# A recurrence followed by an MLP on one core: six weight blocks finished on GpSimd, and a new order of all steps

## The chip, the cores and the metric

The kernel runs on one core of a Trainium2 chip. The core has TensorE for matrix products (PE in the profile; PEld is its loading of weights), VectorE (DVE), ScalarE (ACT), GpSimd (POOL) and SyncE (SP), which here only issues DMAs. Each engine works through its own queue in order and waits on semaphores for the others. The metric is the device time of one execution in microseconds (us), the median of several runs.

## The reference

A recurrence in the manner of RWKV-7 runs over 768 positions for 4 batches and 8 heads with a 40 x 40 state each; its outputs, 3072 tokens of 320 features, go through an MLP with an exact GELU and 2048 hidden features.

```python
for t in range(S):                       # S = 768; state is (B, H, D, D), D = 40
    y[:, :, t] = np.einsum('bhd,bhde->bhe', rt, state)
    Sa = np.einsum('bhde,bhe->bhd', state, at)
    state_decay = state * wt[:, :, None, :] - np.einsum('bhd,bhe->bhde', Sa, bt)
    state = state_decay + np.einsum('bhd,bhe->bhde', vt, kt)
...
x = attn_out.transpose(0, 2, 1, 3).reshape(B * S, H * D)   # 3072 x 320
h = x @ w_in                                               # 320 x 2048
g = 0.5 * h * (1.0 + erf(h * inv_sqrt2))
return (g @ w_out).astype(np.float32)                      # 2048 x 320
```

r, k, v, w, a and b are float32. The two weight matrices arrive as float64 and are read by the kernel as pairs of 32-bit words.

## The kernel before

The sequence is cut into 12 chunks of 64 positions. Within a chunk the recurrence is a set of matrix products and the inverse of a triangular 64 x 64 matrix for each of 32 pairs of batch and head; between chunks only the state is carried on. For chunk c the main steps are: `logs`, `sums` (cumulated logarithms of the decay, and their exponentials), `sc`, `sk` (b and k times weights), `ta`, `tb`, `tk`, `tv`, `tr` (turned operands), the products `N`, `A`, `RV`, each followed by a mask on VectorE (line 676; 703 for chunk 0), the inverse, `av`, `X`, `sa`, `saT`, `M`, and at the end `yy`, `QY`, `qk`, `y` and `state`. Two chunks are under way at any time.

The inverse of chunk 0 is made by squaring (`sq0`, `sq1` for two halves, then `cornerd`, `joinedd`): five rounds, in each of which TensorE multiplies, VectorE transposes (line 865) and adds (868), and ScalarE copies (871). For the other chunks GpSimd inverts 32 x 32 blocks with pairs of short instructions (`inv`, lines 799 and 801), about 26 us of its time for each chunk. It reads N as written to DRAM and loaded back (`nb`), and the result goes through DRAM too (`ft`); `corner` and `joined` put the blocks together.

The MLP of a chunk is `ph` (x times w_in, line 1119, then GELU on ScalarE, line 1122) and `po` (times w_out). For the first two chunks `po` is a plain product (line 1141); from then on it is one level of Strassen's scheme, seven products of half size (line 1157) with sums on VectorE and ScalarE, and two stores of two DMAs each (`store`).

The weights are converted from float64 words in the kernel itself, since the chip computes in float32: ten pieces of w_in (`ci`, 128 x 512 each) and sixteen blocks of w_out (`co`, 128 x 320 each). Each goes through `to_float` (line 452) and one of three buffers `conv0` to `conv2`: VectorE takes the exponent and mantissa bits apart (lines 457 and 458), ScalarE rebiases the exponent (461), VectorE puts the sign in (466), and two more VectorE operations add the low word to the mantissa (472) and multiply by the power (473). The tuples `POOLED_IN` and `POOLED_OUT` name the pieces for which ScalarE scales both parts instead (463, 464) and GpSimd does the addition and the multiplication (469, 470); both are empty before. The words of w_out's blocks 12 and 13 lie in the rows that later hold b and k of a chunk.

Everything that surrounds these steps is set by hand. `ORDER` is a list of tokens such as `ci4:2` or `sq0`. Each step is a generator; a token runs it to its next `yield`, and the numbers after a colon choose its buffers in PSUM (`duo0` to `duo3`) or its conversion buffer. The tokens therefore set the order of instructions in every engine's queue and of the DMAs in SyncE's. The steps of the start are `begin6` (a memset and six products that keep TensorE busy until the first data arrive), `warm0` to `warm7` (a product of constants each), `consts`, `zeros`, `pads` and `gaps` (constants on GpSimd), `tables` (a dummy logarithm or exponential, which has ScalarE load that table) and the loads: `w1` is the load of w for chunk 1, and so on; `wi`, `wl` and `wo` load the weights' words.

Of the kernel before, what the change touches and what calls it, by code (L numbers as in the profile page):

```python
# [33 lines left out]
sq1 sq0 sq1:2 k1 sq0 sq1 warm1:1 N1 sq1 sk0 ci0:0 wi0 sq1:0 N1 ci0 sq1 tr0:1 sq1 ci0 tk0:2 wi0 tk0 sk1 wi0 sq0:3 sq1  # L34
sq0 tr0 A0:2 ci1:1 sq1:0 sq0 ci1 sq1 sq0 nb1 sq1 A0 sq1 wi0 sq0:1 wi0 sq0 RV0:3 sq0 RV0 sq0 wl1 sq1:0 wl1 sq1 inv1 r2
sq0:2 sq1 sq1 sq0 tk1:1 sq0 sq0 sq1:3 tk1 w2 sq1 sq0:0 sq0 cornerd0 placed2 av0:2 ci2:2 placed3 cornerd0:3 ci1 ci2
inv1 nb1 placed1 warm0:1 cornerd0 wl0 ci3:0 wl0 av0 av0:0 r1 ci2 joinedd0:1 av0 joinedd0 tr2:3 placed0 joinedd0 tr2
warm2:2 wi1 a2 ci3 sa0:0 sa0 sa0:1 inv1 sa0 b2 warm5:2 ci4:1 ci9:2 ci4 QY0:3:0 logs2 ci4 k2 qk0 warm7:2 ci9 y0 warm3:1
wi1 state0 wi1 A1:2 wi1 A1 wi1 sums2:1 wi1 inv1 ci9 wo2 sums2:0 sums2 ci3 tv1:3 tv1 tr1:2 sc2 sums2 tn1:0 ci5:1 tn1
ta2:3 ta2 ci5 av1:1 tr1 ci5 sk2 inv1 y0:0 tb2:3 wi1 inv2 ci7:2 tb2 wo6 zeros6 y0:2 ci7 zeros7 y0 y0 tk2:3 av1 ci6:0  # L40
N2:2 ci6 N2 ft1 tk2 co3:1 ph0:0 ft1 ci6 wi1 ph0 corner1:0 N2 ci7 X1:1 corner1:2 corner1 ft1 ph0 X1 ph0:3 wo0 ci8:0
co2:2 ci8 RV1:2 RV1 nb2 warm4:1 ci8 joined1:0 wo9 joined1 wq3 ph0 co0:0 joined1 co0 inv2 ph0 co0 v2 ph0:1 co2 co3
co1:0 sa1:2 co1 sa1 w3 co1 saT1:0 saT1 co3 ph0 co2 wo4 ph0 inv2 ph0:3 co6:0 wt3:1 co6 co7:2 ph0 vp3 co7 ph0 co7
yy1:2:0 logs3 M1:1 M1 tv2:3 wt3 co6 wo8 sums3:1 nb2 sums3 wt3 QY1 zeros5 a3 inv3 tv2 qk1 co4:2 y1 wo15 po0:1 inv2
co5:0 y1 state1 co5 co4 po0 co5 RV2:3 wo10 A2:0 co4 y1 tn2:2 A2 tn2 co9:0 po0 ta3 co9 wt3 inv2 co15:2 bp3 po0 co9 co15
# [5 lines left out]
av3 sums4:1 po1 X3 po1 RV3:2 v4 ws0 sums4 N4:3 N4 inv5 sk4 RV3 ph2:1 N4 sc4 tk4:2 ph2 ft3 ph2 ft3 ph2:3 ws3 nb4 ws1
nb4 ph2 corner3:1 ph2 ft3 ph2:2 inv4 a5 corner3:1 corner3 w5 ph2 ph2 joined3:3 joined3 r4 tn3:1 joined3 tn3 inv4
saT3:3 saT3 sa3:2 sa3 logs5 po1 ph2:1 ta5 bp5 yy3:3:2 M3:0 M3 inv4 tv4 ph2 ph2 tr4 wq5 QY3 qk3 po2:0 po1 sums5:0 sums5
y3 po1 po2:1 state3 y3 po2 inv4 wt5:2 RV4:0 po2:1 po2 wt5 k5 A4:2 po2 A4 tn4:3 y3 tn4 wt5 po2:1 tables1 wt5 po2 po2
inv4 kp5 av4:2 tb5 av4 X4:3 po2 ph3:2 sk5 X4 a6 po2 ta5 ph3 v5 RV4 N5:3 N5 ws2 po2:1 N5 po2 ft4 po2 ph3 ft4 ph3:0 ft4
corner4:0 nb5 tk5:2 ph3 vp5 ph3 corner4:3 ta6 corner4 inv5 nb5 po2 po2:1 po2 joined4:2 joined4 joined4 ph3:0 b5 saT4:3
saT4 sa4:1 r5 inv5 sa4 ph3 ph3 sc5 ph3:2 w6 yy4:3:1 M4:0 M4 tv5 ph3 inv5 ph3 tr5 wq6 QY4 logs6 po3:1 qk4 bp6 state4
po3:0 kp6 y4 po3 po3:2 wt6:0 A5:2 po2 sums6:1 A5 wt6 inv6 k6 inv5 sums6 wt6 y4 po3 wt6 po3 po3:3 po3 po3 tn5:2 y4 tn5
av5:1 tb6 RV5:0 po3 av5 po3 po3:2 ta6 b6 po3 inv5 po3 a7 N6:1 X5:3 N6 X5 N6 sk6 ph4:2 RV5 tk6:1 ph4 ph4 ft5 ta7 ph4:1
ft5 sc6 ft5 A6:3 corner5:0 nb6 r6 inv6 po3 po3:0 po3 corner5:2 A6 corner5 ph4 joined5:0 joined5 ph4 joined5 ph4:2 vp6  # L60
sa5:3 sa5 saT5:0 saT5 inv6 ph4 nb6 ph4 yy5:1:3 w7 M5:0 tr6 tv6 ph4:2 M5 wq7 ph4 inv6 ph4 QY5 v6 logs7 po4:2 qk5 po3 y5
bp7 po4:0 wt7:1 state5 wt7 po4 kp7 po4:0 av6:2 inv7 av6 y5 inv6 wt7 po4 po4 po4:1 wt7 po4 po4 v7 sums7:3 X6:2 y5 po4
ta7 sums7 tb7 po4 po4:0 po4 a8 X6 N7:3 inv6 N7 RV6:1 tk7:2 N7 ph5:2 po4 k7 ph5 ph5 ph5:3 ft6 nb7 ph5 ft6 ph5 nb7
corner6:0 ph5:0 RV6 ft6 inv7 corner6:2 po4 corner6 tn6:3 r7 tn6 po4:1 po4 joined6:2 ta8 joined6 joined6 ph5 inv7 vp7
ph5 sa6:3 sa6 saT6:1 saT6 ph5:2 po4 yy6:0:3 bp8 M6:1 M6 inv7 tr7 ph5 ph5 tv7 QY6 po5:1 wq8 qk6 y6 po5:1 state6 y6 po5
po5:2 inv7 po5 wt8:0 A7:2 y6 RV7:0 A7 wt8 tn7:3 RV7 tn7 wt8 vp8 inv7 po5 po5:1 po5 wt8 po5 X7:2 av7:0 inv8 av7 tb8 sk7
kp8 po5 ta8 b7 inv9 po5 po5:3 po5 a9 po5 N8:0 N8 ft7 ph6:1 N8 ph6 ph6 ft7 ta9 ph6:3 ft7 corner7:1 X7 ph6 tk8:2 nb8 ph6
# [12 lines left out]
N11:1 N11 RV10:2 tk11:1 N11 ph9:3 ft10 RV10 ph9 ft10 ph9 nb11 ph9:0 corner10:0 ft10 sc10 w11 ph9 inv11 ph9 corner10:1  # L80
corner10 po9:2 vp11 po9:2 joined10:3 joined10 joined10 po9 nb11 sa10:0 inv11 sa10 r11 saT10:1 po9:1 saT10 tn10:3 tn10
po9 po9 po9:0 yy10:1:3 v11 M10:2 M10 tv11 po9 inv11 po9 po9 logs11 QY10 qk10 y10 po9 po9:2 y10 state10 po9 po9 X11:0
y10 sums11:1 sums11 A11:3 A11 inv11 po9 po9:2 po9 tn11:1 tr11 tn11 av11:3 po9 av11 RV11:2 X11 b11 inv11 RV11 ph10:1
k11 ph10 ph10 sc11 ph10:3 sk11 ft11 ph10 ft11 ph10 ft11 ph10:0 corner11:0 ph10 ph10 corner11:2 corner11 ph10:1
joined11:3 joined11 joined11 ph10 ph10 saT11:0 saT11 po10:2 po10:2 yy11:3:1 M11:0 M11 po10 po10:1 po10 QY11 po10 qk11
y11 po10:0 y11 po10 po10 y11 po10 y11 po10 po10:2 y11 y11 y11 po10 y11 po10 po10 po10:1 po10 po10 ph11:3 ph11 ph11
ph11:0 ph11 ph11 ph11:2 ph11 ph11 ph11:1 ph11 ph11 po11:0 po11:3 po11 po11:2 po11 po11 po11:0 po11 po11 po11 po11
po11:2 po11 po11 po11 po11:1 po11 po11
"""


@with_exitstack
def kernel(
    ctx: ExitStack,
    tc: tile.TileContext,
    r: bass.AP,
# [12 lines left out]
    nc = tc.nc  # L109
# [3 lines left out]
    C = 64  # L113
# [5 lines left out]
    NCH = S // C  # L119
# [1005 lines left out]
    def half_tile():  # L1125
        return conv().rearrange("p (f t) -> p f t", t=P)

    def store(c, g):
        for e in range(2):
            row = (G * e + g) * S + c * C  # L1130
            nc.sync.dma_start(out=out[row:row + C], in_=oss[g][half(e)].rearrange("p z d -> p (z d)"))

    @step
    def po(c):
# [70 lines left out]
        yield  # L1205
        add(c21, c21, m4)
        yield
        store(c, 1)
        yield


# [56 lines left out]
```

## Time and profile before

| | |
|---|---|
| median of 3 runs | 668.77 us (668.72 to 670.4) |
| profiled execution | 663.67 us, span 661.8 us |
| granted clock of TensorE | 0.999 |
| TensorE busy | 646.7 us (98% of the span) |
| VectorE busy | 416.0 us |
| GpSimd busy | 367.7 us |
| ScalarE busy | 239.3 us |
| idle before TensorE's matmuls in windows 0 to 70 | 7.8 us |
| DMA share, 10 to 60 us | 0.80 to 1.08 |

The page's first part gives each engine's busy time; the second cuts the span into 40 slices of 16.5 us and shows the busy share of each in tenths. In the time line, a row is a group of instructions: its start, its length, the engine, the line of the kernel, what is written and read, the number, and in brackets the idle time just ahead of it with what ended that. A matmul in float32 counts twice, since it runs in two passes. "issue" is idle time in which the engine waited for nothing that the profile shows.

### The profile page before, as it was taken

The page shows a single profiled execution, that of the slowest core. Times are in us where ns is not written, and L with a number is a line of the kernel's source. Part 1 is how long each engine was busy: PE and PEld are TensorE (multiplying, and loading weights), DVE is VectorE, ACT ScalarE, POOL GpSimd, SP SyncE. Part 2 cuts the span into 40 slices and gives each one's busy share as a digit, 9 for nine tenths or more (in the row PEclk, how much of TensorE's full clock was granted, in tenths as well). Part 3 has the DMA queues.
Part 4 walks back from the last instruction along what each step waited for, and adds up shares of the span by engine and source line. Part 5 has one row for each costly group of instructions (what it writes and reads, how often), then busy time and mean ns, then how long its engine had stood idle before and what let it go on. Part 6 is the DMA issues. An engine that isn't in the chain of part 4 may idle for free.

```text
span 661.8 us, 30753 instructions
## 1 busy us (share of the span) xinstructions
PE 646.7 (98%) x13768; PEld 567.3 (86%) x13768; DVE 416.0 (63%) x536; ACT 239.3 (36%) x305; POOL 367.7 (56%) x799
## 2 busy tenths in 40 slices
PE   8889999999999999999999999999999999999997
PEld 4777788777778988998998998998988999998987
DVE  1778989976483874983863963863765674632313
ACT  4355646432424622522522422515253242232020
POOL 6158536706857837846838836847823874840000
PEclk9999999999999999999999999999999999999999
DMA  9989675696676476764775485675685465450100
GB/s 136 164 192 176 158 167 132 153 159 146 116 132 134 105 137 134 140 116 112 145 141 107 94 153 124 119 147 110 115 146 111 103 121 102 86 101 3 42 1 21
DMA packets 300708, 79.41 MB, mean 120 GB/s; under 512 B 288584, under 2 KB 293328, under 8 KB 300576
## 3 DMA queue, kind: packets, MB, share of 16 engines
q1 hardware_dynamic: 299512, 74.92, 58.3%
q0 software_dynamic: 864, 2.36, 1.8%
q8 instruction: 108, 1.77, 1.1%
q14 instruction: 24, 0.20, 0.1%
q10 hardware_dynamic: 200, 0.16, 0.1%
HBM read 64.09 MB, written 9.70 MB: 112 GB/s over the span
## 4 chain that ended last, share of the span: by engine, by line
PE 82%; DVE 8%; SPq 5%; issue 2%; DMA 1%; ACT 0%; DVEq 0%; ACTq 0%
PE duo L1119 29%; PE duo L149 25%; PE duo L1157 22%; PE duo L1141 4%; PE duo L557 2%; SPq L213 2%; SPq L227 1%; DVE conv L466 1%; SPq L1076 1%; DVE conv L472 1%; DMA spare<-in_a_dram 1%; DVE conv L458 1%; DVE conv L457 1%; DVE aT L588 1%; DMA rows<-in_b_dram 0%
## 5 line engine op out<-in xcount | busy, mean ns | idle before, releaser
L1119 PE MATMUL duo<-xt,w_in_sb 64*128 64x256 f32 x1920 | 218.8, 381 | 1.4 <-issue 1.4
L1119 PEld LDWEIGHTS duo<-xt,w_in_sb 64*128 64x128 f32 x1920 | 182.5, 187 | 23.9 <-issue 2.3
L799 POOL TENSOR_TENSOR tmp<-W,Nb 128x56 f32<-128x56 f32 (+22 forms) x155 | 71.8, 464 | 79.9 <-DMA Nb<-N 51.4
L1122 ACT ACTIVATE gt<-duo 128x1024 f32<-128x1024 f32 x48 | 49.2, 1025 | 143.0 <-PE duo L1119 132.1
L799 POOL TENSOR_TENSOR tmp<-rT,Nb 128x56 f32<-128x56 f32 (+22 forms) x155 | 70.2, 453 | 52.8 <-DMA Nb<-N 41.0
L1157 PE MATMUL duo<-w_out_sb,gt 128*128 128x160 f32 x640 | 93.3, 303 | 0.0
L1157 PEld LDWEIGHTS duo<-w_out_sb,gt 128*128 128x128 f32 x640 | 87.6, 190 | 2.4 <-issue 0.8
L801 POOL TENSOR_TENSOR W<-W,tmp 128x56 f32<-128x56 f32 (+22 forms) x155 | 71.8, 463 | 12.1
L801 POOL TENSOR_TENSOR rT<-rT,tmp 128x56 f32<-128x56 f32 (+22 forms) x155 | 68.4, 441 | 12.1
L1157 PE MATMUL duo<-extra,conv 128*128 128x160 f32 x320 | 46.0, 301 | 0.0
L1157 PEld LDWEIGHTS duo<-extra,conv 128*128 128x128 f32 x320 | 43.8, 190 | 1.4 <-issue 0.5
L1141 PE MATMUL duo<-w_out_sb,gt 128*128 128x320 f32 x128 | 36.9, 440 | 0.1
L1161 DVE TENSOR_TENSOR os<-os,duo 128x160 f32<-128x160 f32 x40 | 12.7, 318 | 31.9 <-PE duo L1157 28.0
L1141 PEld LDWEIGHTS duo<-w_out_sb,gt 128*128 128x128 f32 x128 | 23.6, 190 | 10.1 <-issue 0.5
L1164 DVE TENSOR_TENSOR conv<-gt 128x1024 f32<-128x1024 f32 x10 | 12.7, 1266 | 27.5 <-ACT gt L1122 27.5
L605 POOL TENSOR_TENSOR rows<-rows,w_tile 128x640 f32<-128x640 f32 x9 | 15.8, 1761 | 25.0 <-DMA Nb<-N 16.0
L676 DVE TENSOR_TENSOR SM<-duo,left_upper 128x1024 f32<-128x1024 f32 x11 | 13.4, 1221 | 24.4 <-PE duo L149 24.4
L931 DVE COPY Tt<-duo 32x512 f32<-32x512 f32 x11 | 7.6, 689 | 30.4 <-ACT Tt L931 30.3
L149 PE MATMUL duo<-rT,late 40*64 40x64 f32 x1472 | 26.1, 219 | 0.0
L149 PEld LDWEIGHTS duo<-rT,late 40*64 40x64 f32 x1472 | 23.7, 135 | 2.1 <-issue 2.1
L1122 ACT ACT_TABLE_LOAD x14 | 18.0, 1283 | 19.1 <-DVE os L1161 14.7
L1157 PE MATMUL duo<-extra,gt 128*128 128x160 f32 x160 | 23.9, 302 | 0.0
(222 smaller groups left out, 1092.0 us busy)
## 6 DMA issues: line engine op xcount, KB each, us to landing
Nb<-N SPq DMA_DIRECT2D x40, 128.0 KB
VR<-in_v_dram SPq DMA_DIRECT2D x24, 160.0 KB
out_dram<-os SPq DMA_DIRECT2D x48, 80.0 KB
rows<-in_b_dram SPq DMA_DIRECT2D x22, 160.0 KB
rows<-in_k_dram SPq DMA_DIRECT2D x22, 160.0 KB
w_out_sb<-in_moe_w_out_dram SPq DMA_DIRECT2D x5, 640.0 KB
w_tile<-in_w_dram SPq DMA_DIRECT2D x36, 80.0 KB
Tt<-inv SPq DMA_DIRECT2D x44, 64.0 KB
```

What stands on the lines that cost most here:

```text
L149: nc.tensor.matmul(o, lhsT, rhs, start=first, stop=True, skip_group_check=True)
L213: nc.sync.dma_start(out=t[half(e)].rearrange("p g h d -> p (g h) d")[:, :, :D], in_=rows_of(src, c, e))
L557: nc.tensor.transpose(pt[:, g, n], src(g, n), ident)
L605: (nc.gpsimd if c in SCALED_BY_POOL or c >= NB else nc.vector).tensor_tensor(to, raws.pop((c, "k")), t["rw"], ALU.mult)
L676: nc.vector.tensor_tensor(to, pt, upper.unsqueeze(1).to_broadcast([P, NBL, C]), ALU.mult)
L799: eng.tensor_tensor(t, W[:, :nr, j:j + 1].to_broadcast([P, nr, rest]), Nb[:, j:j + 1, j + 1:].to_broadcast([P, nr, rest]), ALU.mult)
L801: eng.tensor_tensor(W[:, :nr, j + 1:], W[:, :nr, j + 1:], t, ALU.add)
L1119: nc.tensor.matmul(pt[:, x, s], w_in_sb[half(x), kt, p * P:(p + 1) * P], xt[half(x), kt], start=kt == 0, stop=kt == NK - 1)
L1122: nc.scalar.activation(gt[:, 4 * q:4 * q + 4].rearrange("p (x s) t -> p x s t", x=2), pt, ACT.Gelu)
L1141: nc.tensor.matmul(pt[:, g], gt[:, f, g * P:(g + 1) * P], w_out_sb[:, f], start=f == 0, stop=f == NF - 1)
L1157: nc.tensor.matmul(pt[:, n, :DM // 2], l_[:, f], r_[:, f], start=f == 0, stop=f == NF // 2 - 1)
L1161: nc.vector.tensor_tensor(to, one_, other, ALU.add)
```

## The change

Four things change together.

1. `POOLED_OUT` names blocks 0, 1, 2, 12, 13 and 14 of w_out, so that their last two operations move from VectorE to GpSimd, with two scalings more on ScalarE for each.
2. `ORDER` is another list. It has the same tokens, but for one more step `warm8`, one more token for each of the six blocks, and one for the last store; nearly every token has another place. Each engine's queue and SyncE's queue of DMAs change with it.
3. Both `tables` steps come earlier: `tables0` (the logarithm) stands at the very start, ahead of the first data; `tables1` among the conversions of w_in.
4. The last two DMAs of the output, one for each half of the rows, are issued by SyncE and by ScalarE instead of both by SyncE.

```diff
-POOLED_IN, POOLED_OUT = (), ()
+POOLED_IN, POOLED_OUT = (), (0, 1, 2, 12, 13, 14)
...
 ORDER = """
-w0 begin6 pads1 consts0 w1 tails1 b1 inv1 zeros1 begin6:0 logs0 zeros2 wi0 gaps0 b0 consts0 logs1 tails0 pads0 a0
-consts0 sums0:1 gaps1 sums0:2 zeros0 v0 sums0 zeros4 warm6:3 pads3 pads2 sums1:0 zeros3 shifts0 sums0 sc0 a1 sums1:3
-sums1 tb0:2 sums1 sc1 wi0 ta0:1 r0 tb0 ta0 tb1:3 N0:0 N0 tb1 wi0 ta1:2 k0 ta1 N0 tv0:1 sq1 v1 tv0 sq0 N1:3 sq0 sq0:0
...
+w1 begin6 zeros0 tables0 tables0 pads1 w0 zeros3 tails1 inv1 zeros1 v0 tails0 gaps0 consts0 begin6:0 logs1 a0 logs0
+consts0 b0 consts0 sums0:1 shifts0 a1 sums0:2 sums0 pads0 sums1:3 zeros2 b1 pads2 sums1:0 sums0 sc0 ta0:2 sums1 r0 ta0
+tb0:1 tb0 warm6:0 N0:2 wi0 sc1 wi0 wi0 N0 tv0:0 k0 tv0 sq0 tb1:1 sq1 sums1 v1 sq1 ta1:0 tb1 ta1 sq0 sq0:3 N1:1 N1 k1
...
+warm8:3 joined3 tn3:1 inv4 ta5 tn3 saT3:2 bp5 saT3 sa3:3 sa3 ph2:0 po1 yy3:1:2 w5 M3:3 M3 inv4 tr4 ph2 ph2 tv4 QY3
...
-    def store(c, g):
-        for e in range(2):
+    def store(c, g, es=(0, 1), eng=nc.sync):
+        for e in es:
             row = (G * e + g) * S + c * C
-            nc.sync.dma_start(out=out[row:row + C], in_=oss[g][half(e)].rearrange("p z d -> p (z d)"))
+            eng.dma_start(out=out[row:row + C], in_=oss[g][half(e)].rearrange("p z d -> p (z d)"))
...
         add(c21, c21, m4)
         yield
-        store(c, 1)
+        if c == NCH - 1:
+            store(c, 1, (0,))
+            yield
+            store(c, 1, (1,), nc.scalar)
+        else:
+            store(c, 1)
         yield
```

More of the change, by code (lines that the diff above doesn't have):

```diff
@@ L36 @@
[L36 to L45, printed above, removed]
@@ L51 @@
[L51 to L55, printed above, removed]
@@ new lines @@
+co13 N3 corner2 po0 co13 co12:0 co13 co12 joined2:1 k3 joined2 co12 po0 co12 joined2 tk3:2 ph1 saT2:2 nb3 saT2 sa2:1
+nb3 sa2 r3 po0 sk3 inv3 po0 po0 yy2:3:2 po0 ta4 b3 M2:1 M2 po0 ph1:0 tv3 inv3 tr3 wq4 ph1 ph1 sc3 po0 QY2 w4 qk2
+state2 po1:1 v3 y2 bp4 po1 ws0 inv3 wt4:1 y2 po1 wt4 po1 logs4 wt4 y2 A3:0 A3 wt4 po1 sums4:2 inv3 av3:3 b4 RV3:0 av3
+tb4 sums4 vp4 po1 ta4 po1 kp4 inv3 po1 po1 N4:3 po1 N4 X3:2 X3 N4 ws1 ph2:1 ws2 v4 inv5 ph2 tk4:0 inv4 ft3 ph2 sk4
+ph2:3 nb4 RV3 nb4 sc4 ph2 ft3 corner3:2 ph2 ft3 ws3 ph2:2 inv4 a5 corner3:1 corner3 r4 ph2 ph2 joined3:0 joined3
@@ L89 @@
+po11 po11:3 po11 po11 po11 po11 po11:1 po11 po11 po11 po11:0 po11 po11 po11
 """
```

88 lines of the change are left out of this document (48 added, 40 removed).

## The prediction

> **What bounds the kernel now.** I read the page's busy shares first, then its forty slices.
>
> ```profile
> PE 646.7 (98%) x13768; PEld 567.3 (86%) x13768; DVE 416.0 (63%) x536; ACT 239.3 (36%) x305; POOL 367.7 (56%) x799
> PE   8889999999999999999999999999999999999997
> DVE  1778989976483874983863963863765674632313
> ```
>
> TensorE is busy 646.7 of 661.8 us, and its slices fall below nine only in the first 50 us and the last slice. So no other engine's work is worth anything in itself: a gain can only be TensorE time taken away (idle, or extra instructions) or time after its last matmul. The time line of TensorE, read for its gaps over 0.2 us, says how much idle there is and what ended it:
>
> ```profile
> 1.54 7.35 PE L149 MATMUL duo<-w_in_sb 128*128 128x512 f32 x12 [1.54 <-DVE w_in_sb L1220]
> 16.36 1.06 PE L557 MATMUL duo<-ident,a_pairs 128*128 128x128 f32 x8 [0.94 <-ACT wpT L525]
> 18.90 1.16 PE L149 MATMUL duo<-aT,nT 40*64 40x64 f32 x64 [0.61 <-DVE aT L588]
> 20.48 1.06 PE L557 MATMUL duo<-ident,spare 128*128 128x128 f32 x8 [0.42 <-DMA spare<-in_a_dram]
> 36.49 1.45 PE L149 MATMUL duo<-w_in_sb,Nb 64*64 64x96 f32 x29 [1.00 <-ACT w_in_sb L871]
> 42.19 0.87 PE L149 MATMUL duo<-w_in_sb,Nb 64*64 64x96 f32 x14 [1.08 <-issue]
> 55.19 1.37 PE L149 MATMUL duo<-N,Tt 64*64 64x104 f32 x25 [0.58 <-DVE Tt L902]
> 69.34 1.09 PE L149 MATMUL duo<-ident,VR 128*64 128x128 f32 x16 [1.05 <-issue]
> 138.23 1.16 PE L149 MATMUL duo<-aT,nT 40*64 40x64 f32 x64 [0.23 <-DVE aT L588]
> 143.20 1.34 PE L1119 MATMUL duo<-xt,w_in_sb 64*128 64x256 f32 x9 [1.41 <-issue]
> 207.18 1.16 PE L149 MATMUL duo<-Tt,avs 64*64 64x64 f32 x62 [0.59 <-DVE Tt L931]
> 238.54 1.16 PE L149 MATMUL duo<-aT,nT 40*64 40x64 f32 x64 [0.38 <-DVE aT L588]
> ```
>
> The bracket is the idle time and what ended it. With three smaller gaps (0.27 issue, 0.37 for a copy at L871, 0.25 issue) they come to 10.7 us. An order of steps can remove those that end on a row of DVE, ACT or a DMA: 3.92 us up to 55.19 (0.94, 0.61, 0.42, 0.37, 1.00, 0.58) and 1.20 us later (0.23, 0.59, 0.38). The "issue" gaps, 4.06 us, wait for nothing that the profile shows; I let them stay. The 1.54 before the warm-up matmuls stays too: those run to 8.89 and cover the first loads, logarithms and constants. After 238.54 there is no gap until the last product, whose chain is:
>
> ```profile
> 642.20 15.42 PE duo L1157 x112
> 657.62 0.02 issue
> 657.64 0.32 DVE os L1161
> ```
>
> From 657.64 to the span's end is 4.1 us: one addition, the stores and their landing. Last, the windows by stage, to see who is full where TensorE is not:
>
> ```profile
> 30.00:40.00 10.00, 9.00 (x270) 8.65 (x271) 9.66 (x15) 4.89 (x7) 2.87 (x6) 1.00 0.80 197
> 60.00:70.00 10.00, 8.95 (x257) 6.77 (x251) 9.93 (x16) 4.94 (x6) 8.67 (x18) 1.00 0.94 220
> 130.00:140.00 10.00, 9.77 (x197) 8.59 (x196) 9.86 (x19) 4.38 (x5) 1.66 (x5) 1.00 1.04 209
> ```
>
> Columns after the length: PE, PEld, DVE, ACT, POOL, granted clock, DMA share, GB/s. VectorE is full from 25 to 140, beside a TensorE that is nearly full, and the clock is full.
>
> The sum is made against this execution's 663.67 us (its span and 1.9 around it); the median of the three runs is 668.77, 5.1 above, and I carry the difference over. What a measurement can tell from no change is about 0.3%, 2.0 us.
>
> **The conversions.** Two VectorE operations of a block of w_out (L472, 0.48 to 0.94 us; L473, 0.49 for 128x320) go for six blocks: 6 x (0.49 + 0.49) = 5.9 us less on VectorE. ScalarE gets two scalings each; its nearest rows are a copy of 128x320 at 0.43 and L461 at 0.56, so 12 x 0.5 = 6 us, on an engine that is 36% busy. GpSimd gets an addition and a multiplication each: the rows of tensor_tensor there are 1.54 for 128x640 (L605) and 0.24 for 128x31, so 320 elements take 0.24 + 289 x 2.13 ns = 0.86, and twelve 10.3 us. GpSimd idled 16.8 us before inverse 2 and 16.0 before the next; in the new order three blocks lie after the eighth row of inverse 2, delaying the rest of it 5.2 us, and three ahead of inverse 3. All this lies at 80 to 150 us, where the only gap that ends on VectorE is 0.23. So 5.9 us on VectorE buy **-0.2** (bounds -0.2 and, through the next paragraph, +4). Its cover is the matmuls of L1119 and L1141 queued around it.
>
> What the trace shows against it is that VectorE waits while GpSimd works:
>
> ```profile
> 32.00 1.61 POOL L605 TENSOR_TENSOR extra<-rT,SM 128x640 f32<-128x640 f32 x1 [3.27 <-DMA w_out_sb<-in_moe_w_in_dram]
> 32.24 1.93 DVE L473 SCALAR_TENSOR_TENSOR w_in_sb<-conv 128x512 f32<-128x512 f32 x1
> 71.61 1.74 POOL L605 TENSOR_TENSOR extra<-rows,w_tile 128x640 f32<-128x640 f32 x1
> 71.86 2.24 DVE L458 TENSOR_SCALAR conv<-gt 128x512 uint32<-128x512 uint32 x1
> ```
>
> L473 takes 0.69 elsewhere and L458 0.42; they lost 1.24 and 1.82 to one GpSimd instruction each. Priced so, twelve instructions cost VectorE at most 12 x 0.86 = 10.3 us and at least nothing (an operation that reads one input from PSUM, like L676, kept its 1.2 us beside GpSimd), so its balance lies between -5.9 and +4.4. [...]
>
> VectorE also gets a new wait: a conversion buffer is now given back by GpSimd, so three later conversions' first operations (L457) stand behind GpSimd's multiplications, and the additions and masks queued after them with it. By my chain GpSimd ends the first of those near 92 to 95 us, when VectorE arrives there; what TensorE next needs from behind it (the mask of M1) lies some ten operations later. I take nothing.
>
> **The head.** The new order loads w1, w0, v0, a0, b0, a1, b1, then r0 and w_in. In the trace the first two transfers have landed at 5.62 and the fifteenth (spare) at 20.34: (20.34 - 5.62) / 13 = 1.13 us each, one behind the other. So b0, now the tenth, lands near 5.62 + 8 x 1.13 = 14.7 (it was the ninth), a0 near 12.4 instead of 15.8, and b1, now the fourteenth, near 19.2 (it was the sixth). b0 x weights on VectorE (0.83) ends 15.6, flips (1.06) 16.7, the copy (1.02) 17.8: the first product N0 runs at 17.8 instead of 18.90. But its mask (L703) stands behind b1 x weights on VectorE, 19.2 + 0.83 = 20.1, against 20.19 now: nothing gained there. From the mask to the last transpose of the inverse by squaring (46.62) VectorE's time line has 4.5 us idle (0.35, 0.54, 0.30, 1.67, 1.06, 0.57) and 1.24 in the blocked L473; the new order adds the a1 product (1.23) and one more pair of L457 and L458 (0.8) to this stretch. With no idle left the end comes 4.5 + 1.2 - 2.0 = 3.7 earlier, with all of it left 2.0 later. Followed row by row, the later conversions fill the waits of the rounds and it ends 1 to 2.5 earlier. On TensorE this can be worth at most the 3.92 us of gaps up to 55.19; I take **-1.6** (bounds -3.9 and +2.0), nearer to the good end since the chain's gaps at 36.49 and 55.19, 1.58 us, end on exactly these rounds.
>
> **Tables ahead.** A table load is 1.28 us on ScalarE; there are 44 before and 41 after, and the first now precedes the data. It was at 5.62, but TensorE starts the sums at 8.83 behind the warm-up in either case. Nothing; without that cover, -1.28.
>
> **The rest of the order.** TensorE's sequence alternates among kinds 206 times instead of 200. A group of 20 matmuls of L1119 by itself takes 2.36 in the chain and 40 take 4.52, so a change costs 0.20 there; 64 of L149 take 1.09 and 128 take 2.02, 0.16. Six more: **+0.9** (0 to 1.2). One more warm-up step (warm8, two matmuls of 0.53, 1.06 us) stands at joined3, just where TensorE waited 0.59 at 207.18: **+0.5** (0.4 to 1.06). Of the gap at 238.54 I take half: **-0.2** (-0.4 to +0.4; every chunk's steps have moved, and a gap of that size may open anywhere).
>
> **The last store.** The four last DMA issues of SyncE fill 2.57 us from 656.53, the fourth from 658.5. With the fourth on ScalarE's queue it starts after the addition, at 658.0: **-0.5** (-0.6 to 0; ScalarE's own issues at L1076 took 0.60, the first 1.29).
>
> Sum: -0.2 - 1.6 + 0.9 + 0.5 - 0.2 - 0.5 = -1.1, so 662.6 for the profiled execution and **667.7** for the median.
>
> **The rivals.** *The head gains all that it can*: the squaring rounds close up and TensorE's gaps to 55.19 go, 3.9, with the later ones, 1.0, and the groups cost only half: -3.9 - 0.2 - 0.6 + 0.5 + 0.4 - 0.6 = -4.4, 664.4. For it speak the 4.5 us that VectorE idled between full windows; against it, that b1 arrives late. *VectorE is held by GpSimd* (slower): VectorE runs at 9.9 of 10 from 110 to 140 and TensorE already waits for it at 138.23, so from there any lateness is TensorE's. At the bad balance, +4.4, instead of -0.2: -1.1 + 0.2 + 4.4 = +3.5, 672.3. It decides as soon as GpSimd costs VectorE more than the 5.9 saved, half a microsecond for each of the twelve. Against it: the new instructions follow each other in two blocks, and much of VectorE's work there reads PSUM. *The rounds run late*: two inputs of this head now come near their need, and if b1 lands one or two transfers later the mask, the rounds and all behind them shift, +2.0 instead of -1.6: +2.5, 671.3.
>
> **How the numbers follow.** Forecast (-2.9 to +1.0 around -1.1): 0.47. Full gain (-2.9 and below): 0.28. GpSimd holds VectorE: 0.15. Rounds late: 0.10. A tenth of a chance inside the forecast lies below -2.0, so faster by over 0.3% is 0.38, within 0.3% 0.37, slower 0.25. The range leaves out a tenth on each side: 663.6, a little under the full gain since an issue gap or two may go with it, to 672.2, near the bad balance.
>
> **What would show it.** Right: N0's matmuls near 17.8, L703 near 20, the squaring's last transpose (L876) near 45, TensorE's gaps to 55 at about 2 us, no gap over 0.3 ending on VectorE from 80 to 150, the two L470 blocks at about 0.86 each, last issues under 2.1 us. Wrong: operations of VectorE over 1.2 us beside L469 and L470 with a TensorE gap behind them; L703 after 21; or new TensorE gaps behind 150, where I gave the new order nothing to lose.

## The result, and the profile after

The changed kernel took 671.93 us (median of 17 runs, 669.36 to 676.06), the kernel before 668.29 beside it (17 runs, 664.42 to 674.74): a ratio of 1.0059 (95% interval 1.0038 to 1.0081), 3.9 us slower. Two later comparisons on other occasions gave 1.0059 (1.0028 to 1.0090) and 1.0065 (1.0035 to 1.0094). The prediction had 1.1 us faster. The time lies in its range, on the wrong side.

First the page's busy shares and two of its forty-slice rows.

```profile
PE 653.6 (98%) x13770; PEld 569.8 (85%) x13770; DVE 412.5 (62%) x524; ACT 239.2 (36%) x314; POOL 379.1 (57%) x811
PE   9899899999999999999999999999999999999997
DVE  1799679995574863972882882962764773542303
PEclk9999899999999999999999999999999999999999
```

TensorE's busy time has risen by 6.9 us, to 653.6, and the granted clock dips in the fifth slice. VectorE's fell by 3.5 only. TensorE's larger gaps, from its time line as before:

```profile
17.61 1.16 PE L149 MATMUL duo<-aT,nT 40*64 40x64 f32 x64 [0.24 <-ACT nT L620]
24.36 1.16 PE L149 MATMUL duo<-aT,nT 40*64 40x64 f32 x64 [0.40 <-DVE aT L588]
31.80 1.45 PE L149 MATMUL duo<-w_in_sb,Nb 64*64 64x96 f32 x29 [1.09 <-ACT w_in_sb L871]
69.33 1.97 PE L557 MATMUL duo<-ident,st 128*128 128x128 f32 x8 [2.76 <-POOL st L379]
71.09 1.72 PE L557 MATMUL duo<-ident,a_pairs 128*128 128x128 f32 x8
114.05 1.66 PE L149 MATMUL duo<-SM,extra 64*64 64x104 f32 x64 [1.35 <-DVE SM L676]
143.47 1.16 PE L149 MATMUL duo<-aT,nT 40*64 40x64 f32 x64 [0.43 <-DVE aT L588]
304.11 0.74 PE L149 MATMUL duo<-conv,spare 32*32 32x32 f32 x64 [1.30 <-DVE conv L908]
345.56 1.16 PE L149 MATMUL duo<-aT,nT 40*64 40x64 f32 x64 [1.14 <-DVE nT L614]
```

The first three lie in the head; N0 at 17.61 is as forecast. In this execution the issue gaps of 1.08, 1.05 and 1.41 are gone, and so are the waits at 207 and 238. In their place stand waits that the profile of the kernel before did not show: 2.76 us at 69 for the memset of the state's padding (L379), 1.35 at 114 for a mask, 1.30 and 1.14 at 304 and 346. The two rows behind the longest hole are slow too: eight flips take 1.97 and 1.72 us, against 1.04 before. The windows (columns as before: length, PE, PEld, DVE, ACT, POOL, granted clock, DMA share, GB/s) show why:

```profile
60.00:65.00 5.00, 4.96 (x185) 3.87 (x180) 4.33 (x8) 2.82 (x4) 4.45 (x8) 1.00 0.90 178
65.00:70.00 5.00, 2.24 (x27) 1.51 (x20) 4.56 (x7) 1.63 (x2) 4.45 (x10) 0.91 0.99 233
70.00:75.00 5.00, 5.00 (x34) 4.00 (x33) 1.92 (x3) 1.50 (x2) 4.06 (x14) 0.75 0.39 122
```

The granted clock fell to 0.75 behind the hole. VectorE, nearly full here before, idles in the same window (1.92 of 5.00 busy): it waited 3.32 us, up to 72.92, for these flips. GpSimd's time line says why the memset was late:

```profile
67.43 0.70 POOL L799 TENSOR_TENSOR rows<-os,rows 128x96 f32<-128x96 f32 x1
68.20 0.71 POOL L801 TENSOR_TENSOR os<-os,rows 128x96 f32<-128x96 f32 x1
68.86 0.41 POOL L379 MEMSET st<- 128x384 f32 x1
69.24 0.58 POOL L799 TENSOR_TENSOR rows<-os,rows 128x91 f32<-128x91 f32 x1
```

The step `zeros4`, which stood far ahead of inverse 1 before (its memset ran at 10.56 us), is now one memset among inverse 1's rows on GpSimd's queue; and inverse 1 began 3.0 us later (41.36 against 38.35).

### The profile page after: what moved, and what is told of

Same layout as the page of the kernel before. It is cut to its first block, busy times and chain, and to the rows that moved or that the text cites. A ratio compares the mean times of both kernels' runs of the same rounds, so it can differ in the third digit from the quotient of the medians.

```text
span 670.2 us, 30773 instructions
## 1 busy us (share of the span) xinstructions
PE 653.6 (98%) x13770; PEld 569.8 (85%) x13770; DVE 412.5 (62%) x524; ACT 239.2 (36%) x314; POOL 379.1 (57%) x811
## 4 chain that ended last, share of the span: by engine, by line
PE 75%; DVE 8%; POOL 5%; SPq 4%; DMA 4%; issue 3%; ACT 1%; DVEq 0%; POOLq 0%
PE duo L1119 25%; PE duo L149 22%; PE duo L1157 21%; PE duo L1141 4%; PE duo L557 2%; POOL os L801 2%; POOL rows L799 2%; SPq L224 1%; SPq L715 1%; DMA Nb<-N 1%; DVE conv L466 1%; DVE conv L544 1%; DVE conv L458 1%; DMA N<-spare 1%; DVE conv L472 1%
## 5 line engine op out<-in xcount | busy, mean ns | idle before, releaser
L799 POOL TENSOR_TENSOR tmp<-W,Nb 128x56 f32<-128x56 f32 (+22 forms) x155 | 74.3, 479 | 59.3 <-DMA Nb<-N 47.5
L799 POOL TENSOR_TENSOR tmp<-rT,Nb 128x56 f32<-128x56 f32 (+22 forms) x155 | 70.1, 452 | 56.8 <-DMA Nb<-N 45.1
L801 POOL TENSOR_TENSOR W<-W,tmp 128x56 f32<-128x56 f32 (+22 forms) x155 | 69.4, 448 | 12.1
L1141 PE MATMUL duo<-w_out_sb,gt 128*128 128x320 f32 x128 | 37.0, 440 | 0.0
L1141 PEld LDWEIGHTS duo<-w_out_sb,gt 128*128 128x128 f32 x128 | 23.5, 190 | 9.9 <-POOL W L801 0.5
L461 ACT ACTIVATE conv<-conv,rebias 128x320 uint32<-128x320 uint32 (+1 forms) x26 | 15.8, 620 | 24.5 <-DVE conv L457 24.4
L605 POOL TENSOR_TENSOR rows<-rows,w_tile 128x640 f32<-128x640 f32 x9 | 14.7, 1630 | 14.9 <-DMA rows<-in_k_dram 7.2
```

The costliest lines, as they stand in the source:

```text
L461: nc.scalar.activation(power, power, ACT.Relu, bias=rebias, scale=8.0)
L605: (nc.gpsimd if c in SCALED_BY_POOL or c >= NB else nc.vector).tensor_tensor(to, raws.pop((c, "k")), t["rw"], ALU.mult)
L799: eng.tensor_tensor(t, W[:, :nr, j:j + 1].to_broadcast([P, nr, rest]), Nb[:, j:j + 1, j + 1:].to_broadcast([P, nr, rest]), ALU.mult)
L801: eng.tensor_tensor(W[:, :nr, j + 1:], W[:, :nr, j + 1:], t, ALU.add)
L1141: nc.tensor.matmul(pt[:, g], gt[:, f, g * P:(g + 1) * P], w_out_sb[:, f], start=f == 0, stop=f == NF - 1)
```

## The experiments

All ratios are to the kernel before on the same chip. Kernels 1 to 4, 5 to 8, 9 to 12 and 13 to 15 each shared a chip and its runs of the kernel before; 16 ran alone.

**1. The padding early.** The changed kernel, `zeros4` ahead of inverse 1.

```diff
-... sums2:0 state0 zeros4 sums2:2 inv1 ...
+... sums1:3 zeros2 zeros4 b1 ...   (and: sums2:0 state0 sums2:2 inv1)
```

> The changed kernel with one step moved back: the zeroing of the state's padding (L379) stands before inverse 1 on GpSimd instead of inside it. Theory A (TensorE waits for that memset behind inverse 1, and runs at half speed after it): the gap of 2.76 us at 69.33 goes and with it the slow matmuls behind it (1.97 and 1.72 us for eight where 1.04 is usual, about 1.7 us): 4 to 4.5 us less than the changed kernel, ratio to before near 0.999. Theory B (GpSimd's conversions hold VectorE and so TensorE): the memset is beside the point, ratio stays near 1.006. Theory C (the steady chunks of the new order have gaps of their own, 1.30 at 304 and 1.14 at 346): stays near 1.004 or above.

1.0056 (1.0027 to 1.0086). The gap of 2.76 went, but TensorE then waited 1.39 at 68.33 for the state itself (L1089), and 0.61, 0.38 and 0.82 from 87 to 95 for inverse 1's result, with the clock at 0.5 to 0.8 from 95 to 99. The longest hole was not by itself the loss.

**2. No block pooled.** `POOLED_OUT = ()` in the changed kernel.

> The changed kernel with the six blocks converted on VectorE again, in the new order. Theory A: the gap at 69.33 stays; VectorE has 5.9 us more to do between 90 and 150 and the gap before the chunk-1 state mask (1.35 at 114) grows by up to 2: ratio 1.006 to 1.009. Theory B: VectorE is let go and the ratio falls to about 1.00.

1.0060 (1.0016 to 1.0103): the order is as slow without GpSimd's conversions. Its page also says what pooling is worth to VectorE in this order:

```profile
PE 653.9 (98%) x13770; PEld 569.9 (85%) x13770; DVE 412.3 (62%) x536; ACT 234.8 (35%) x302; POOL 365.6 (55%) x799
```

VectorE is busy 412.3 us with all conversions and 412.5 without the twelve operations. The fall by 3.5 against the kernel before is the order's, not pooling's.

**3. Pooling alone, in the old order.** `POOLED_OUT` as changed, the third token of each of the six blocks doubled, nothing else.

> The kernel before with the six blocks finished on GpSimd and nothing else changed. Theory A: within 0.3% of before (-0.2 to +0.5 us, as predicted for this part). Theory B: +2 to +4.4 us, ratio 1.003 to 1.007, with gaps of TensorE that end on VectorE between 95 and 150.

1.0084 (1.0055 to 1.0113). Here the wait that the prediction took at nothing is the largest of all. VectorE's time line:

```profile
93.79 0.50 DVE L466 SCALAR_TENSOR_TENSOR conv<-w_out_sb,conv 128x320 uint32<-128x320 uint32 x1
102.95 0.33 DVE L457 TENSOR_SCALAR conv<-w_out_sb 128x320 uint32<-128x320 uint32 x1 [8.66 <-POOL w_out_sb L470]
```

TensorE's, a little later:

```profile
105.24 0.33 PE L149 MATMUL duo<-rT,turned 40*64 40x64 f32 x2 [1.13 <-ACT SM L968]
106.21 1.14 PE L149 MATMUL duo<-rT,turned 40*64 40x64 f32 x60 [0.65 <-ACT late L981]
111.46 3.68 PE L149 MATMUL duo<-ident,VR 128*64 128x128 f32 x32 [3.15 <-ACT gt L1122]
```

VectorE stood 8.66 us for a conversion buffer, because GpSimd's addition and multiplication lay behind eight rows of inverse 2. ScalarE's next rebias (L461) stood behind VectorE, and the copies and the GELU that TensorE needs stood behind that rebias.

**4. The last store on two queues, alone**, in the kernel before.

> The kernel before with the last two stores issued by SyncE and ScalarE. Both theories: -0.5 us (0 to -0.6), too little for the ratio to tell; the span from the last addition's end to the end of the span shrinks from 3.8 to about 3.3 us.

1.0016 (0.9986 to 1.0046), undecided as a time. In the profile the part is plain: from the start of the last addition to the span's end it took 3.88 us (660.32 to 664.2), 4.16 before (657.64 to 661.8), 3.82 in the changed kernel. So -0.3 us. This run is also a second profile of the old order, and is used as one below.

**5. N1's stores first.** The changed kernel, the stores of N1 (L715) ahead of three loads on SyncE.

```diff
-N1:1 N1 k1 ... wi0 sq0 wi0 pads3 sq1:1 sq0 gaps1 N1 sq1
+N1:1 N1 N1 k1 ... wi0 sq0 wi0 pads3 sq1:1 sq0 gaps1 sq1
```

> The changed kernel with one step moved: the four stores of N1 (L715) stand on SyncE's queue ahead of the loads of k for chunk 1 and of two pieces of w_in, where in the changed kernel they stood behind them (mask ended 26.85, stores issued 30.95). Theory A, that inverse 1 started late by this and made TensorE wait for it (the memset queued behind its rows at 66 to 69, or its result at 87 to 94): the stores are issued at 27.5, inverse 1 starts near 38 instead of 41.36 and ends near 71.5 instead of 74.9, the gap of 2.76 at 69 shrinks to under 0.6, the granted clock stays over 0.95 from 65 to 75, no gap over 0.7 from 85 to 97; ratio to the kernel before 1.000 (0.997 to 1.003). Rival B, that the new order loses in many places and another dependency stops TensorE next: a gap of 2 us or more elsewhere before 110, ratio 1.005.

1.0070 (1.0051 to 1.0090). The stores were issued at 27.26 instead of 30.95, but inverse 1 began at 40.80, not near 38: the load that brings N1 back (L784) now stood right behind four loads of w_in, and GpSimd got its bytes 5.4 us after the last of its two issues. In this execution the wait on the padding was shorter (1.11 at 68), but 0.67 stood at 92 and 1.69 at 112, and the time did not fall. Theory A fails, though inverse 1 did not begin as early as it asks.

**6. The mask of M1 first as well**, ahead of one block's last three operations and the next block's first two on VectorE.

```diff
-ph0 co7 co7 vp3 ph0 yy1:1:3 wt3 M1:2 co4:1 M1
+ph0 co7 vp3 ph0 yy1:1:3 wt3 M1:2 M1 co7 co4:1
```

> As the run with N1's stores first, and the mask of M1 (L676, SM) stands on VectorE's queue ahead of three operations of one block's conversion and two of the next, where it was behind them and TensorE waited 1.35 us for it at 114.05. Theory A with the mask as second cause: the gap at 114 goes (under 0.3), what stood behind it (L466, L472, L473 of that block) comes 1.2 later and nothing on TensorE waits for it; ratio 0.998 (0.995 to 1.001). Rival B: the wait comes back within 30 us at the conversions or the next mask, ratio the same as without this move.

1.0106 (1.0086 to 1.0126), the highest ratio of all. The wait at 114 went and came back 10 us later at the conversions that had been passed:

```profile
124.61 0.81 PE L1141 MATMUL duo<-w_out_sb,gt 128*128 128x320 f32 x2 [0.62 <-DVE w_out_sb L473]
126.39 3.83 PE L1141 MATMUL duo<-w_out_sb,gt 128*128 128x320 f32 x8 [0.97 <-DVE w_out_sb L473]
```

The window behind it, of the same execution:

```profile
126.00:130.00 4.00, 3.61 (x8) 2.37 (x9) 3.98 (x7) 1.12 (x2) 3.29 (x9) 0.66 0.12 25
```

The clock fell to 0.66, and eight matmuls of L1141 took 3.83 us, where 128 take 36.9 us in the kernel before, 2.3 for eight.

**7. The old order, N1's stores late**: behind two more loads of w_in on SyncE.

> The kernel before with one step moved: N1's four stores stand behind two more loads of w_in on SyncE's queue (29.25 before, about 31.6 here). Theory A: inverse 1 starts near 40.7 instead of 38.35 and ends near 74, TensorE waits 1 to 3 us for chunk 1's corner or what follows it between 84 and 97, ratio 1.003 (1.001 to 1.006). Rival B: the old order has enough slack there, no gap over 0.7 from 84 to 97, ratio 1.000.

1.0070 (1.0047 to 1.0093), but not by what theory A named. Inverse 1 began at 41.62 and ended at 76.3, and no gap over 0.3 stands from 84 to 97. TensorE waited 1.06 at 78 for a product on GpSimd (L605) that stood behind inverse 1's last rows, but run 4, in the old order, waited 0.78 there. It lost at 121 (1.01) and 155 (0.89) on w_out's conversions and at 143 in an issue gap of 1.72 with the clock at 0.5 behind it. Why two loads passed by one store do so much there stays open.

**8. Pooling in the old order, ahead of inverse 2**: the first `inv2` with rows moved behind the first three pooled blocks.

> The old order with the six pooled blocks (as in the run with the pooled blocks alone, where VectorE stood 8.66 us from 94.3 for a conversion buffer that GpSimd returned behind eight rows of inverse 2), with those eight rows moved behind the first three blocks on GpSimd. Theory C, that the whole cost of pooling in the old order was that wait on GpSimd's queue: VectorE's wait at 94 falls under 2.5 us, the gaps of 1.13, 0.65 and 3.15 at 105 to 111 go, inverse 2 ends a few us later but no gap over 1 follows from it; ratio 1.001 (0.998 to 1.004). Rival D, that GpSimd's work on SBUF slows VectorE and that is the cost: VectorE's operations beside L469 and L470 take over 1 us and the ratio stays at 1.006 or more.

1.0098 (1.0077 to 1.0119). VectorE's wait of 8.66 shrank to 1.85, as theory C had it, but the next three blocks made VectorE wait 4.43 at 146.5 for GpSimd's addition, and TensorE stood 1.41 at 122, 1.93 at 141 and 1.31 at 150, besides 1.64 at 77 for GpSimd's L605 and 1.46 at 87. Theory C falls: curing the first wait moved it to the second group of blocks.

**9 to 11. The new order in parts.** The two orders have executed almost the same steps at two places, near 66 and 165 us (they differ there by the steps `tables`, one load and waits of GpSimd's). So each stretch was taken from the new order with the other two old, none pooled, the old last store. In 10 and 11 PSUM buffers were renamed so that the stretches join.

```diff
9:  new[:198] + old rest
10: old[:195] + new[198:401] + old rest
11: old[:395] + new rest (with warm8)
```

> The kernel before, with the new order for the first 198 steps alone (to about 66 us: loads, sums, the inverse by squaring, the state after chunk 0), then the old order of all other steps; no block pooled, the old last store. Theory E, that the head's own gain is about as predicted but the store of N1 and the state's padding queued behind inverse 1 give back more: TensorE is 1 us ahead at 60, then a gap of 2 to 3 us on the state near 69 with the granted clock under 0.9 behind it; ratio 1.004 (1.001 to 1.007). Rival F, that the loss sits in the steps behind 66 us: ratio 0.998.

> The kernel before, with the new order for the steps of about 66 to 165 us alone (chunk 1 and the conversions of w_out, without pooling). Theory E: 1 to 2 us slower from gaps on VectorE's masks and copies at 105 to 150, ratio 1.002 (1.000 to 1.005). Rival F: most of the change's loss is here, ratio 1.005 or more.

> The kernel before, with the new order for the steps behind about 165 us alone, with the new warm-up step at joined3, without pooling and with the old last store. By the terms of the prediction: 0.9 for six more changes among kinds of matmuls and 0.5 for the step, +1.4, ratio 1.002. Theory G, that the new order is worse than that behind 165 us because the waits at 304 and 345 belong to it: +3 us, ratio 1.005 (1.003 to 1.007), with two gaps of 0.4 us or more between 300 and 360.

Head 1.0006 (0.9971 to 1.0041), middle 1.0039 (1.0010 to 1.0069), rest 1.0019 (0.9991 to 1.0047): +0.4, +2.6 and +1.3 us. The middle's interval alone excludes no change. In 9 the gap on the padding that theory E expects did not come (the old order behind the head needs the padding later, and only an issue gap of 0.37 stands at 69); in 11 one wait of over 0.4 stood between 300 and 360 (0.78), so theory G's two did not come either. The middle's gaps in the profile:

```profile
67.27 1.09 PE L557 MATMUL duo<-ident,st 128*128 128x128 f32 x8 [2.12 <-ACT w_tile L522]
92.38 0.88 PE L149 MATMUL duo<-Tt,Js 32*32 32x32 f32 x60 [0.97 <-DMA Tt<-inv]
111.70 1.66 PE L149 MATMUL duo<-SM,extra 64*64 64x104 f32 x64 [0.91 <-DVE SM L676]
141.87 1.16 PE L149 MATMUL duo<-aT,nT 40*64 40x64 f32 x64 [1.12 <-DVE aT L588]
```

The waits at 112 and 142 are at the places of the changed kernel's. The first is not: the padding is early here, and the 2.12 us are a wait for a PSUM buffer that my renaming made. The middle's +2.6 thus holds a wait that the changed kernel does not have, and lacks the one on the padding. Its mean granted clock is also 0.9956 over its executions, against 0.9977 for the kernel before beside it; by my estimate the difference, 0.0021 of 669 us, costs 1.4. So the +2.6 is not a clean measure of what the changed kernel loses there.

**12. The changed kernel beside the parts.**

> The changed kernel itself once more, beside the three part orders on one chip. If the parts add up, its ratio less one is the sum of theirs within 0.003; measured before 1.0059 (1.0038 to 1.0081). The gap of 2.76 on the state's padding at 69 with the granted clock at 0.5 to 0.8 for 4 us behind it is there again if it is fixed by the order; if it is a matter of one execution's timing it is not.

1.0059 (1.0028 to 1.0090); the parts add up to 1.0064, with the middle as it is, in part by luck. The gap on the padding was there (2.80 at 69.53, the clock at 0.5 behind it), and those at 114.63 (1.35), 307.89 (1.15) and 345.49 (1.16).

**13 to 15. Both GpSimd waits early, with and without pooling, and the changed kernel beside them.** 13 has the moves of 1 and 5 together; 14 is 13 with `POOLED_OUT = ()`; 15 is the changed kernel.

> The changed kernel with both of the late things of the stage from 60 to 100 us taken early: N1's stores ahead of three loads on SyncE, and the memset of the state's padding ahead of inverse 1 on GpSimd. TensorE's, VectorE's and ScalarE's orders are those of the changed kernel. Theory A2, that these two waits with the slower clock behind them are what the middle loses (2.6 us by the part order alone): no gap over 0.8 from 60 to 100, the clock at 0.98 or more there, ratio 1.002 (1.000 to 1.004), and at least 0.003 below the changed kernel's on the same chip. Rival B, that the middle's loss comes back at VectorE, which is full from 105 to 147: TensorE's gaps from 105 to 150 sum to 3 us or more, ratio within 0.002 of the changed kernel's.

> As the run with the stores and the padding early, with no block pooled. By the prediction's term pooling is worth 0.2 us: the same ratio within 0.002. If VectorE's stage from 105 to 147 is what binds once the waits ahead of it are gone, the 5.9 us of VectorE's time that pooling saves show here: 2 us or more slower than with pooling, ratio higher by 0.003 or more, and TensorE's gaps on VectorE from 105 to 150 longer by as much.

> The changed kernel on the same chip as the two that differ from it, for the difference alone: ratio 1.006 (1.004 to 1.008); its gap of 2.8 at 69 on the padding is fixed by the order and there again.

1.0062 (1.0028 to 1.0095), 1.0066 (1.0035 to 1.0097) and 1.0065 (1.0035 to 1.0094): one time for all three. In 13 no gap over 0.6 stood from 60 to 105, and nothing was gained, so theory A2 falls. Without pooling the time is the same too, as the term of the prediction had it. Each interval is about 0.3% to either side, so differences under 2 us are not told apart. VectorE is busy 414.5 us in 13 and 413.6 in 14: here too pooling takes nothing from it. The profile of 15 is instructive in itself: its span was 664.6 us, 5.6 less than in the first profile of the same kernel, with the same wait on the padding but the clock at full speed behind it:

```profile
68.34 1.09 PE L557 MATMUL duo<-ident,st 128*128 128x128 f32 x8 [1.94 <-POOL st L379]
112.08 1.66 PE L149 MATMUL duo<-SM,extra 64*64 64x104 f32 x64 [1.61 <-DVE SM L676]
340.80 1.16 PE L149 MATMUL duo<-aT,nT 40*64 40x64 f32 x64 [1.17 <-DVE nT L614]
```

and on its page

```profile
PE 649.6 (98%) x13770; PEld 567.2 (85%) x13770; DVE 412.1 (62%) x524; ACT 239.2 (36%) x314; POOL 377.3 (57%) x811
```

**16. Inverse 1 really early.** As 13, with L784 two loads of w_in earlier on SyncE.

```diff
-... tk0 sq0:3 wi0 sk1 ci0 wi0 sq0 ... tr0:3 sq1 ci0 sq1 nb1 sq0:0
+... tk0 sq0:3 nb1 wi0 sk1 ci0 wi0 sq0 ... tr0:3 sq1 ci0 sq1 sq0:0
```

> As the run with N1's stores and the padding early, and the load that brings N1 back for GpSimd (L784) two loads of w_in earlier on SyncE. In the two runs with the stores alone moved, they were issued 3.7 us earlier, but L784's bytes took 5.4 us or more to land behind four loads of w_in and inverse 1 began at 40.8 and 41.7, no earlier than in the changed kernel (41.4). Theory A, tested properly: L784 issued by 33 with two loads ahead, inverse 1 begins by 37.5 and ends by 71.5, no wait on its result from 85 to 97, ratio 1.003 or less. Rival B, that the changed order's loss is spread (a wait per stage, and TensorE's own 2.9 us of extra instructions and changes of kind): inverse 1 is early and the ratio stays at 1.005 to 1.007.

1.0067 (1.0031 to 1.0104). Inverse 1 began at 39.85 and ended at 74.0, later than hoped; in three executions of the changed kernel it began at 40.66 to 41.36 and ended at 74.9 to 75.2. Nothing on TensorE waited for it or for the padding from 60 to 105, and the time stayed. Inverse 1 did not begin by 37.5, as theory A asks, but no wait was left that an earlier start could remove. Rival B holds: neither of these waits carries the loss.

## Why the prediction was wrong

**Where the time went.** I add up TensorE's idle time from the time lines by stage, without the 1.54 at the start; "waits" end on a row, "issue" on nothing shown. Old: the kernel before, run 4, and run 11 up to 165 us. New: three executions of the changed kernel (first profile, runs 12 and 15).

| us | old | new | change of the mean |
|---|---|---|---|
| waits, 2 to 60 | 3.92, 2.47, 3.72 | 2.84, 4.13, 3.30 | 0.0 |
| waits, 60 to 105 | 0, 0.78, 1.02 | 2.76, 2.80, 2.26 | +2.0 |
| waits, 105 to 165 | 0.23, 1.14, 0.76 | 1.78, 2.15, 1.61 | +1.1 |
| waits, 165 to 290 | 0.97, 1.35 | 0, 0, 0 | -1.2 |
| waits, 290 to the end | 0, 0.32 | 2.44, 2.84, 1.17 | +2.0 |
| issue, all | 4.06, 4.40 | 0.44, 0.30, 0.80 | -3.7 |

So idle time as a whole hardly changed (+0.2). These are few executions, and the other runs say which rows to trust. The waits from 60 to 165 us stand in every execution of the changed kernel. Those behind 165 do not separate the orders: five executions of the old order there (before, 4, 7, 9, 10) waited 1.0 to 3.1 us, 1.9 on the mean, and eleven of the new one (the three, 1, 2, 5, 6, 11, 13, 14, 16) 0.3 to 2.8, 1.4 on the mean. Nor do the issue gaps belong to the order alone: with the changed kernel's order of TensorE they come to 0.3 to 3.5 us in ten executions (1.4 on the mean), with the old one to 0.7 to 4.4 in five (before, 3, 4, 7, 8; 2.9).

TensorE's busy time rose. The changed kernel's order of TensorE with no dip of the clock before the last product has 649.6, 650.5, 650.7 and 652.4 us (runs 15, 5, 14, 16), the old order 646.7 and 648.0 (before, run 4): +3.4 between the means, with 2.8 between executions of one order. Of this, 1.2 us are two more matmuls, seen in every execution (below). The rest is not shown to be the order's: run 9, with the old order behind the head and no dip either, has 651.0. 3.4 + 0.2 - 0.3 for the store is +3.3. Measured were +3.9 to +4.3.

Where the clock dips behind a hole, 1 to 3 us come on top by my estimate (from the 3.5 us of 16 flips against 2.0 at full clock, and the lengths of the dips, 3 to 7 us, both below), but that is not the loss either. Among the executions with a mean granted clock of 0.999 or more, the changed kernel beside 13 and 14 takes 668.8 us (mean of 5) and the kernel before 664.3 (17); beside the parts it is 671.3 (2) against 667.7 (18).

**The step that failed** is the sum's idle time. It had -2.6 of idle (-1.6 in the head, -0.2 at 138, about -0.6 at joined3 and -0.2 at 238) and nothing lost elsewhere. Both halves were off. In the head, the step was that the later conversions fill the waits of the squaring rounds, so that these end 1 to 2.5 us earlier. VectorE's time line has their last transpose in the kernel before, in run 4 (the old order again) and in the changed kernel:

```profile
46.62 0.71 DVE L876 STREAM_TRANSPOSE W<-w_in_sb 128x512 f32<-128x512 f32 x1
45.19 0.71 DVE L876 STREAM_TRANSPOSE W<-w_in_sb 128x512 f32<-128x512 f32 x1
45.95 0.71 DVE L876 STREAM_TRANSPOSE W<-w_in_sb 128x512 f32<-128x512 f32 x1
```

Six executions share the old head (before, 3, 4, 8, 10, 11): the transpose stands at 44.35 to 46.62, 45.1 on the mean, and the profile from which I predicted is the latest of them. Five share the new head (the changed kernel's three, 2, 9): 45.38 to 45.98, 45.8 on the mean. The rounds end 0.7 us later, not earlier, though the mask ahead of them (L703) comes 0.4 earlier: the stretch from mask to transpose takes 26.3 us instead of 25.1. That the work which the new order adds to it was not hidden in its waits is the likely reason, not a tested one. Elsewhere, new waits came where I gave the order nothing to lose: 1.9 to 2.8 us on the padding near 69 and 1.35 to 1.6 on the mask at 112 to 115, in all three executions. What the rest of the loss is made of stays open.

Term by term:

- **Conversions, -0.2: right as a time, not in its mechanism.** 13 against 14 and 2 against the changed kernel show nothing either way, within about 2 us. GpSimd's durations were right for the most part (0.86 to 1.08 for ten of the twelve, but 1.21 and 1.73 for one block). The 5.9 us less on VectorE were not: the mechanism of the rival *VectorE is held by GpSimd* is in the trace, and it ate the saving. VectorE's time line, changed kernel:

```profile
99.40 0.49 DVE L466 SCALAR_TENSOR_TENSOR conv<-w_out_sb,conv 128x320 uint32<-128x320 uint32 x1 [1.81 <-ACT conv L461]
102.18 0.99 DVE L457 TENSOR_SCALAR conv<-w_out_sb 128x320 uint32<-128x320 uint32 x1 [0.77 <-POOL w_out_sb L470]
103.09 1.02 DVE L458 TENSOR_SCALAR conv<-w_out_sb 128x320 uint32<-128x320 uint32 x1
104.04 1.16 DVE L466 SCALAR_TENSOR_TENSOR conv<-w_out_sb,conv 128x320 uint32<-128x320 uint32 x1
105.12 0.31 DVE L457 TENSOR_SCALAR conv<-w_out_sb 128x320 uint32<-128x320 uint32 x1
```

  Beside L469 and L470 the same operation takes 0.99, with GpSimd between instructions 0.31: 0.7 lost. L466, which reads two tiles in SBUF, takes 1.16 here and 0.49 at 99.40. In the new order VectorE's busy time is the same with and without pooling (412.5 and 412.3; 414.5 and 413.6), so its balance was about nothing, well inside the bounds -5.9 and +4.4. In the old order pooling took 1 to 4 us from it (412.5 and 413.9 in runs 3 and 8, 415.1 to 416.6 without). L457 and L458, which read one tile, took 0.99 and 1.02 beside them; why VectorE waits there, no run shows. The new wait for a conversion buffer is 0.77 in the new order; in the old order it was 8.66 (run 3).
- **Head, -1.6: wrong in its mechanism.** The rows up to the mask came near the forecast: N0 at 17.61 (17.8), L703 at 19.32 (20.1). The rounds behind it did not close up, as shown above. TensorE's waits up to 60 us are 2.5 to 3.9 in the six executions with the old head (3.4 on the mean) and 2.8 to 4.1 in the five with the new (3.2), so there was next to nothing of the 3.92 to gain. b0 and b1 come later now, and in runs 12 and 15 a gap of 1.3 to 1.7 opened at 16 us behind b0's product, a milder form of the rival *rounds run late*. Timed alone the head gives +0.4 (-1.9 to +2.7), which does not exclude -1.6 by itself.
- **Six changes of kind and the new step, +1.4: low.** Busy time says +3.4. Two more matmuls of cum_m by ident, in groups that rose from 8.5 to 9.7 us, are 1.2 of it, and no wait stood at 207 in the changed kernel's three executions; the remaining 2.2 are above my bound of 1.2 for the six changes, though not by more than executions differ. The rest of the order timed alone, with this step, gave +1.3 (-0.6 to +3.1).
- **The gap at 238, -0.2:** it went wholly.
- **The store, -0.5:** -0.3, inside the bounds.

**What filled the middle.** The wait on the padding was to be foreseen: `zeros4` moved to between two `inv1` tokens, and the prediction did not follow the moved memset along GpSimd's queue nor N1's stores along SyncE's. Yet taking either away gained nothing (1, 5, 13, 16). A reading that fits: VectorE idles at most 1.0 us from 105 to 120 and 0.7 from 120 to 140 in any run; in the 55 us ahead of that (50 to 105) it idled 5.1 and 7.5 us in the old order (before, run 4), where I had called it full, and 11.9, 12.7 and 11.0 in the changed kernel. So it comes to the stretch in which it is full with more left to do, and a wait mended ahead brings TensorE sooner to VectorE, as run 6 shows for one case. This is argued, not shown: runs 2 and 14 do not test it, since VectorE's busy time is the same in them as with pooling, and no run of this order takes work from VectorE there.

## What to carry to other kernels

In a kernel whose bounding engine is 98% busy, a reordering is not priced by the gaps that it closes: follow every moved instruction past each queue it passes, memsets and DMA stores too, and expect new waits of the size of those closed. Take the gaps from more than one execution before counting them as gain; here the end of the squaring rounds lay anywhere from 44.35 to 46.62 us in six executions of one order, and the prediction was worked out from the latest. Read a busy engine's saving from its busy time with and without the change in the same order, since here the order alone moved VectorE's by as much. When mending one wait after another leaves the time where it is, time the parts of the change against each other rather than the waits.

## What the runs showed of the hardware

**The clock fell behind some short holes, and their length alone does not decide.** Holes of 2.76 and 2.80 us (changed kernel), 2.77 (run 2), 3.15 (run 3), 1.72 (run 7) and 1.93 (run 8) were followed by 3 to 7 us at about half the granted clock (0.52 from 69 to 71 us in the first profile of the changed kernel), and so were two holes of 0.62 and 0.97 within 2.4 us (run 6); holes of 2.12 (run 10), 1.94 (run 15) and 1.69 (run 5) were not. In run 13 the clock fell behind a hole with no visible cause, 2.15 us long, as its time line shows:

```profile
43.88 0.87 PE L149 MATMUL duo<-w_in_sb,Nb 64*64 64x96 f32 x14 [2.15 <-issue]
44.68 1.52 PE L557 MATMUL duo<-ident,extra 128*128 128x128 f32 x8
```

In the windows behind it the clock is 0.65 and 0.50, though TensorE is busy all the time:

```profile
44.00:48.00 4.00, 4.00 (x58) 3.55 (x58) 1.02 (x2) 1.50 (x2) 3.28 (x10) 0.65 0.80 103
48.00:52.00 4.00, 4.00 (x62) 4.00 (x62) 3.50 (x8) 1.81 (x3) 3.38 (x9) 0.50 1.18 190
```

The 16 flips behind the hole took 3.5 us (69.33 to 72.81) in the first profile of the changed kernel, and 2.0 (68.34 to 70.31) at full clock in run 15; that a dip costs 1 to 3 us is my estimate from this and from the lengths above. The clock fell behind 1.72 us in run 7 and not behind 2.12 us in run 10; what decides it, no run shows.

**One order, 5.6 us between profiles.** The first profile of the changed kernel and that of run 15 differ by 670.2 to 664.6 in span, most of it by the clock behind one hole and by two waits behind 290 us. A term of 1 us read from one profile is within that.

**Issued earlier, landed hardly earlier.** In three executions of the changed kernel the load that feeds inverse 1 (L784) was issued from 35.93, 37.03 and 37.32, behind two loads of w_in, and GpSimd began 2.8 to 3.6 us after the last issue, at 40.66 to 41.36. In runs 5 and 13 it was issued from 33.45 and 33.50, right behind four loads of w_in, and GpSimd began 5.4 and 7.0 us after the last issue, at 40.80 and 41.66. With two of the four put behind it (run 16) it was issued from 33.42 and took 5.3 us, to 39.85. So how many loads stand just ahead does not explain the time. The DMA share from 32 to 42 us was 0.94 to 1.04 in these three runs, and 0.63 to 0.96 in the first profile of the changed kernel; that the bytes ahead held the load up is a reading that fits, not shown.
